# Turning the key-value sums: one transposition and two copies in place of two products and one copy

## The chip, the cores and the metric

The kernel runs on one core of a Trainium2 chip. A core has a matrix engine (TensorE, PE in the profile, with PEld for its weight loads), a vector engine (DVE), a scalar engine (ACT), GpSimd (POOL) and queues that start transfers (SP among them). The metric is the device time of one execution in microseconds (us), as the median of several. A profiled execution has besides a span, from the first to the last instruction of the program; everything read from the profile is measured inside that span.

## The reference, cut to what matters

Four batches, four heads, 1088 tokens, head dimension 32. Attention uses a feature map of 64 products (8 x 8) in place of a softmax, and the result goes through a two-layer network with an exact GELU:

```python
def phi(x):                       # 32 numbers -> 64 features
    a, b = S1 @ x, S2 @ x         # 8 and 8
    return outer(a, b).reshape(64)

kv  = einsum('bhsf,bhsd->bhfd', phi(k), v)      # 64 x 32 for each batch and head
z   = phi(k).sum(axis=tokens)
num = einsum('bhsf,bhfd->bhsd', phi(q), kv)
den = einsum('bhsf,bhf->bhs',  phi(q), z) + 1e-6
x   = (num / den)                               # heads side by side: 4352 x 128
out = gelu_exact(x @ w_in) @ w_out              # 128 -> 2048 -> 128
```

The change concerns `kv` of batches 1 to 3 between its summation and its use in `num`. No number that the reference defines is left out or altered.

## The kernel before, in words

The tokens are cut into nine pieces: for each batch two of 512 tokens (pieces 0 to 7), and one that gathers the last 64 tokens of every batch. For each piece the kernel computes query features, then the attention output, then for 16 slices of 128 hidden channels the first layer (L721), the GELU (L728, on ACT) and the second layer (L807). Most of the second layer is computed with a scheme that takes 7 products in place of 8; GpSimd forms sums of its inputs at L772 to L775, and L807 multiplies them.

In this long stage a hidden slice is two products (L721), one for 64 output channels each. The first writes PSUM partitions 0 to 63, the second 64 to 127, so each uses one half of the array's columns, and the two run side by side. The products of the second layer come in pairs in the same way. In the profile such products have the form 128\*64 (rows of weights by columns of weights); a product on the whole array has the form 128\*128. Each float32 product appears as two records, each with a weight load of its own; a transposition through the matrix engine (L333, L702) appears as one.

The key-value sums of batch b (1 to 3) are formed by `kv_sum` (L437), 128 rows (head and value channel) by 64 columns (features). `take_kv` (L462) copies them to SBUF as `kv_T[b]`. `turn_kv` then turns them: the result `kz[b]` has the features in the rows, twice, in rows 0 to 63 and again in rows 64 to 127, because the two halves of the tokens are multiplied from different rows in `attend_products` (L633). Before the change each copy of the turned block is a product of its own, with `kv_T[b]` as the weights and the identity matrix as the other operand: one product for PSUM partitions 0 to 63, one for 64 to 127. One ACT copy (L468) takes all 128 rows to `kz[b]`.

`turn_kv` runs three times, for batches 1, 2 and 3, some 3 to 20 us after the copy to `kv_T`. The order of all work is written out by hand: the loop over `steps` emits one hidden slice, then whatever `slots[t]` holds for this step (there `turn_kv` sits), then the second layer's products of `products[t]`. At the end of the program every instruction is tied to the one before it on its engine, so each engine keeps the order of the text. On PE, `turn_kv` stands between a pair of L721 and a pair of L807 in all three cases; on ACT, its copy stands between two GELUs. PSUM for hidden slices (`hps`) has two banks, the banks of `turn_kv` come from `wps`, two buffers of two banks each. `kz[b]` is read next by the products of L633, several us later.

Batch 0 goes another way (L930, a copy alone) and is not touched.

Of the kernel before, what the change touches and what calls it, by code (L numbers as in the profile page):

```python
# [16 lines left out]
def kernel(  # L17
# [18 lines left out]
    pe, dve, act, pool, sp = nc.tensor, nc.vector, nc.scalar, nc.gpsimd, nc.sync  # L36
    B, H, S, D = q.shape
    R = S1.shape[0]
    F = R * R
# [27 lines left out]
    def work_banks():  # L67

        return wps.tile([128, 2, CW], FP, name="w_ps")
# [10 lines left out]
    def out_bank():  # L80
        return ops.tile([128, CW], FP, name="o_ps")
# [137 lines left out]
    ident = big.tile([128, 128], FP, name="ident")  # L219
# [8 lines left out]
    kz = [big.tile([128, 128], FP, name=f"kz{b}") for b in range(B)]  # L228
# [229 lines left out]
    kv_T = {}  # L458
# [4 lines left out]

    def turn_kv(b, banks):

        for rows in (slice(0, 64), slice(64, 128)):
            pe.matmul(banks[rows, 1, :128], lhsT=kv_T[b], rhs=ident, start=True, stop=True)  # L467
        act.copy(out=kz[b], in_=banks[:, 1, :128])  # L468


    S_ab = big.tile([128, 2, 2 * R], FP, name="S_ab")
# [436 lines left out]
    banks = [out_bank(), out_bank()]  # L908
# [174 lines left out]
    at(24, kv_and_attend, 1, 1)  # L1083
    at(24, query_sketch, 2)
    at(26, lambda: turn_kv(1, held["kv"]))
    at(24, query_outer, 2)
    for i, t in enumerate((25, 26, 28)):
# [3 lines left out]
    for n in range(3, NCHUNK):  # L1091

        t = (n - 1) * NF
        b = (n + 1) // 2 if n % 2 else n // 2
        keys = n % 2 and b < B
        if n == NMAIN - 2:
            for m in (n, n + 1, NMAIN):
                at(t - 6, query_turn, m)
            at(t - 1, last_sketches, b)
            for i in range(2):  # L1100
                at(t + 6 + 3 * i, query_outer, n + i)
            at(t + 11, lambda b=b: turn_kv(b, work_banks()))
            at(t + NF - 1, last_attends)
# [4 lines left out]
        if keys:  # L1108
            at(t - 1, sketch_and_attend, n)
            at(t - 1, features_of_all, b)  # L1110
        else:
            if n % 2 == 0 and b < B:
                at(t - 1, z_sum, b)
                at(t - 1, fold_z, b)
                at(t - 1, kv_and_attend, b, n - 1)
                at(t + 1, lambda b=b: turn_kv(b, held["kv"]))
            else:
                at(t - 1, attend, n - 1)
            at(t - 1, query_sketch, n)
# [16 lines left out]
    for t, (n, fi) in enumerate(steps):  # L1136
# [13 lines left out]
        elif fi % NB == NB - 1:  # L1150
            b = fi // NB
# [11 lines left out]
    for t in range(len(steps) + LAG):  # L1163
        if t < 4:
# [9 lines left out]
            if t == 3:  # L1174
                banks = work_banks()
# [26 lines left out]
        if t < len(steps) and steps[t][0] < NMAIN and steps[t][1] % NB == NB - 1:  # L1202
            n, b = steps[t][0], steps[t][1] // NB
# [50 lines left out]
```

## Time and profile before

| what | value |
|---|---|
| time, median of 3 executions | 259.25 us (259.1 to 259.41) |
| span of the profiled execution | 257.9 us |
| granted TensorE clock over the span | 0.999 |
| L467, products of `turn_kv` | 12 records, 272 ns each, three places: 60.7, 103.0 and 176.1 us |
| L468, the ACT copy of `turn_kv` | 3 records, 259 ns each |
| L462, the ACT copy to `kv_T` | 3 records, 217 ns each |
| L721 on PE | 514 records, 136.9 us busy |
| L728 on ACT, blocks of 4 slices | 128 records, 73.1 us busy |

The span is shorter than the time by 1.4 us, which lie before the first and after the last instruction. A record of a matrix product is longer than the distance to the next one, since products are pipelined: its duration has the way through the array in it. What a product costs the engine is therefore read from the distance between starts, or from the chain of waits, which counts each stretch once. In the forms, "128\*64 128x512 f32" is a product with 128 rows and 64 columns of weights that 512 columns stream through. A merged row ("x4") covers several records that follow each other.

### The profile page before, as it was taken

To read this page: it belongs to the slowest core of one execution; us is meant where nothing else is said; L and a number is where in the kernel's file an instruction comes from. 1 tells how busy PE (TensorE), PEld (TensorE's weight loads), DVE (VectorE), ACT (ScalarE), POOL (GpSimd) and SP (SyncE) were. 2 spreads that over 40 slices of the span, in tenths; PEclk is the share of its full clock that TensorE was granted. 3 is DMA by queue.
4 is the path that set the end of the run, shared out by engine and by line. 5 is a ranking of instruction groups with operands and counts; after the bars stand their busy time and mean duration, and the time that the engine had idled before them with its cause. 6 is when DMAs were issued, how large, how long until landed. Compare 5 with 4: busy or idle time off the path is not lost.

```text
span 257.9 us, 5770 instructions
## 1 busy us (share of the span) xinstructions
PE 253.1 (98%) x2335; PEld 135.5 (53%) x2335; DVE 151.1 (59%) x313; ACT 115.2 (45%) x224; POOL 163.6 (63%) x173
## 2 busy tenths in 40 slices
PE   8989999999999999999999999999999999999995
PEld 7846444354444545444444455455544444445794
DVE  3786888969699997590178986399307000700330
ACT  4665777433626332543335332533444334433442
POOL 3313006799968778587758775787758777877300
PEclk9999999999999999999999999999999999999999
DMA  6459747751000101102000002000200200020020
GB/s 203 143 156 375 181 117 174 211 131 15 4 0 13 29 3 23 20 8 35 3 0 3 0 10 37 0 1 3 41 3 5 38 0 1 7 36 0 3 41 20
DMA packets 29594, 13.48 MB, mean 52 GB/s; under 512 B 21888, under 2 KB 27776, under 8 KB 29568
## 3 DMA queue, kind: packets, MB, share of 16 engines
q1 hardware_dynamic: 29392, 13.05, 20.2%
q8 instruction: 18, 0.29, 0.5%
q10 hardware_dynamic: 176, 0.07, 0.1%
q14 instruction: 8, 0.07, 0.1%
HBM read 10.88 MB, written 2.23 MB: 51 GB/s over the span
## 4 chain that ended last, share of the span: by engine, by line
PE 93%; SPq 2%; DMA 2%; DVE 1%; issue 0%; ACT 0%
PE h_ps L721 45%; PE o_ps L807 33%; PE o_ps L858 5%; PE w_ps L855 3%; DMA small<-in_moe_w_in_dram 2%; PE w_ps L437 1%; PE w_ps L578 1%; PE w_ps L633 1%; SPq L132 1%; PE h_ps L737 1%; SPq L100 1%; PE w_ps L977 1%; PE w_ps L656 0%; SPq L118 0%; PE w_ps L467 0%
## 5 line engine op out<-in xcount | busy, mean ns | idle before, releaser
L721 PE MATMUL h_ps<-xT,w_in 128*64 128x512 f32 (+3 forms) x514 | 136.9, 576 | 0.0
L728 ACT ACTIVATE block<-h_ps 128x512 f32<-128x512 f32 (+1 forms) x128 | 73.1, 571 | 117.2 <-PE h_ps L721 115.3
L721 PEld LDWEIGHTS h_ps<-xT,w_in 128*64 128x64 f32 (+1 forms) x514 | 41.9, 142 | 30.5 <-issue 11.6
L807 PE MATMUL o_ps<-block,w_out 128*64 128x256 f32 x224 | 57.5, 379 | 0.0
L772 POOL TENSOR_TENSOR bits_low<-block 128x512 f32<-128x512 f32 x28 | 36.0, 1286 | 27.7 <-ACT block L728 27.7
L807 PEld LDWEIGHTS o_ps<-block,w_out 128*64 128x64 f32 x224 | 30.5, 137 | 38.0 <-issue 27.5
L773 POOL TENSOR_TENSOR bits_a<-block 128x512 f32<-128x512 f32 x28 | 35.8, 1278 | 11.8 <-ACT block L728 11.8
L822 DVE COPY sums<-o_ps 64x256 f32<-64x256 f32 x8 | 3.3, 417 | 60.6 <-PE o_ps L807 60.6
L774 POOL TENSOR_TENSOR bits_e<-bits_a,block 128x512 f32<-128x512 f32 x28 | 36.1, 1288 | 2.2
L775 POOL TENSOR_TENSOR bits_m<-block,bits_e 128x512 f32<-128x512 f32 x28 | 35.9, 1282 | 2.2
L807 PE MATMUL o_ps<-bits_a,small 128*64 128x256 f32 x112 | 28.8, 379 | 0.0
L807 PE MATMUL o_ps<-bits_low,small 128*64 128x256 f32 x112 | 28.8, 379 | 0.0
L807 PE MATMUL o_ps<-block,small 128*64 128x256 f32 x112 | 28.8, 379 | 0.0
L807 PE MATMUL o_ps<-bits_m,w_out 128*64 128x256 f32 x112 | 28.7, 379 | 0.0
L807 PEld LDWEIGHTS o_ps<-block,small 128*64 128x64 f32 x112 | 15.2, 137 | 17.9 <-issue 10.8
L807 PE MATMUL o_ps<-bits_e,small 128*64 128x256 f32 x112 | 17.0, 383 | 0.0
L858 PE MATMUL o_ps<-g,w_out 128*128 128x512 f32 (+1 forms) x34 | 16.5, 572 | 0.0
L807 PEld LDWEIGHTS o_ps<-bits_m,w_out 128*64 128x64 f32 x112 | 15.3, 137 | 0.0
L807 PEld LDWEIGHTS o_ps<-bits_a,small 128*64 128x64 f32 x112 | 15.2, 137 | 0.0
L807 PEld LDWEIGHTS o_ps<-bits_low,small 128*64 128x64 f32 x112 | 15.2, 137 | 0.0
L590 DVE STREAM_TRANSPOSE w_ps<-w_ps 128x512 f32<-128x512 f32 (+1 forms) x7 | 4.8, 687 | 17.1 <-ACT xT L644 12.7
L807 PEld LDWEIGHTS o_ps<-bits_e,small 128*64 128x64 f32 x112 | 7.7, 137 | 10.6 <-issue 8.8
(195 smaller groups left out, 303.7 us busy)
## 6 DMA issues: line engine op xcount, KB each, us to landing
block<-in_moe_w_in_dram SPq DMA_DIRECT2D x3, 512.0 KB, 11.3
block<-in_moe_w_out_dram SPq DMA_DIRECT2D x3, 512.0 KB, 14.7
k<-in_k_dram SPq DMA_DIRECT2D x12, 128.0 KB, 2.9
v<-in_v_dram SPq DMA_DIRECT2D x12, 128.0 KB, 3.5
q<-in_q_dram SPq DMA_DIRECT2D x24, 64.0 KB, 2.1
out_dram<-oT SPq DMA_DIRECT2D x21, 64.0 KB, 2.2
k<-in_k_dram SPq DMA_DIRECT2D x2, 256.0 KB, 2.8
q<-in_q_dram SPq DMA_DIRECT2D x2, 256.0 KB, 3.9
```

The lines of the kernel that those rows point to most:

```text
L100: eng.dma_start(out=main[n, b][:, heads], in_=src_of[n][b, heads, 0:MAIN, :].rearrange("h (p j) d -> p h j d", j=J))
L590: dve.transpose(out=tok, in_=ps[:, :, :H2])
L721: pe.matmul(ps[rows, :W], lhsT=w[:, rows], rhs=xT[n][:, :W], start=True, stop=True)
L728: act.activation(out=g_of[n, fi][:, :W], in_=ps[:, :W], func=ACT.Gelu)
L772: pool.tensor_sub(out=s[3], in0=a11, in1=a21)
L773: pool.tensor_add(out=s[1], in0=a21, in1=a22)
L774: pool.tensor_sub(out=s[2], in0=s[1], in1=a11)
L775: pool.tensor_sub(out=s[4], in0=a12, in1=s[2])
L807: pe.matmul(acc[n][bank][half * 64:(half + 1) * 64, col:col + HW], lhsT=fixed, rhs=moving, start=opens and e == 0 and name in "4715", stop ...
L822: dve.tensor_copy(out=N[lo, 0, one], in_=a0[lo, one])
L855: pe.matmul(o_of[n][i][:, :128], lhsT=g[:, i * 128:(i + 1) * 128], rhs=w_tile(w_out_sb, fi), start=first, stop=final)
L858: pe.matmul(o_of[n][:, cols], lhsT=w_tile(w_out_sb, fi), rhs=g[:, cols], start=first, stop=final)
```

## The change

`turn_kv` makes the turned block once, by a transposition through the matrix engine into PSUM partitions 0 to 63, and ACT copies it twice, to rows 0 to 63 and to rows 64 to 127 of `kz[b]`. F is 64.

```diff
     def turn_kv(b, banks):
 
-        for rows in (slice(0, 64), slice(64, 128)):
-            pe.matmul(banks[rows, 1, :128], lhsT=kv_T[b], rhs=ident, start=True, stop=True)
-        act.copy(out=kz[b], in_=banks[:, 1, :128])
+        pe.transpose(banks[:F, 1, :128], in_=kv_T[b], identity=ident)
+        for rows in (slice(0, F), slice(F, 2 * F)):
+            act.copy(out=kz[b][rows], in_=banks[:F, 1, :128])
```

The places of the calls, their order on the engines, the banks and the transfers stay as they were. On PE two products become one transposition at each of the three places; on ACT one copy of 128 x 128 becomes two of 64 x 128. In the program as built, a product of 64 weight columns names two of the array's four groups of 32 columns; the transposition, with 64 weight columns too, names all four, as the transpositions of 128 columns do. It has one weight load and one matrix instruction.

## The prediction

> **What bounds the kernel now.** I read the page first, for the bound:
>
> ```profile
> span 257.9 us, 5770 instructions
> PE 253.1 (98%) x2335; PEld 135.5 (53%) x2335; DVE 151.1 (59%) x313; ACT 115.2 (45%) x224; POOL 163.6 (63%) x173
> PE 93%; SPq 2%; DMA 2%; DVE 1%; issue 0%; ACT 0%
> ```
>
> PE is busy for 98% of the span and makes up 93% of the chain that ended last. In the 40 slices of the span its digit is 9 (90% or more) from the fourth to the last but one, so what is taken from its stream or put into it should reach the end one for one. ACT, at 45%, has room. Next the chain of waits around the first turn, 58 to 64 us (start, us, what):
>
> ```profile
> 59.18 0.86 PE o_ps L807 x8
> 60.04 0.86 PE h_ps L721 x4
> 60.90 0.22 PE w_ps L467 x4
> 61.12 0.86 PE o_ps L807 x8
> ```
>
> The turn, four records, costs 0.22 us of the chain. That is two passes of 0.11 us: the two products lie on different column halves and run side by side. The chain around the other turns has the same 0.22. No time is lost on either side, since L721, L467 and L807 all have the form 128\*64.
>
> The third view is PE's timeline where that form changes (96.2 to 100.6 us), and the chain there:
>
> ```profile
> 96.67 1.03 PE L721 MATMUL h_ps<-xT,w_in 128*64 128x512 f32 x4
> 97.63 0.32 PE L437 MATMUL w_ps<-k_s,ones 128*32 128x64 f32 x8
> ...
> 99.34 0.64 PE L578 MATMUL w_ps<-qT,S_abc 64*32 64x256 f32 x16
> 99.91 0.65 PE L807 MATMUL o_ps<-bits_e,small 128*64 128x256 f32 x4
> 100.39 0.60 PE L721 MATMUL h_ps<-xT,w_in 128*64 128x512 f32 x2
> ```
>
> ```profile
> 99.55 0.43 PE w_ps L578 x16
> 99.98 0.58 PE o_ps L807 x4
> ```
>
> A block of four L721 records takes 0.86 in the chain, so L437 could start at 96.67 + 0.86 = 97.53; it starts at 97.63. I read the 0.10 us as the array running empty before it takes another division of its columns. After L578, the four records of L807 cost 0.58 in the chain, where eight cost 0.86 and so four 0.43: 0.15 us more. Of these, 0.05 is the first weight load, which nothing hides (99.91 to 100.39 is 0.48, not 0.43; a first L807 record is 430 ns where the median is 379), and 0.10 is the emptying again.
>
> Last, transpositions, by line and in the timeline:
>
> ```profile
> L333 PE MATMUL w_ps<-ident,q x4: 272/272/328, 10.9 to 11.2; 128*128 128x128 f32 x4
> L333 PE MATMUL o_ps<-ident,k_rem x1: 328/328/328, 8.5 to 8.5; 128*128 128x128 f32 x1
> ```
>
> ```profile
> 8.52 0.33 PE L333 MATMUL o_ps<-ident,k_rem 128*128 128x128 f32 x1
> 8.78 0.66 PE L426 MATMUL o_ps<-sums,k_p 128*64 128x33 f32 x16
> ...
> 21.41 0.38 PE L702 MATMUL w_ps<-ident,x_tok 128*128 128x128 f32 x2
> 21.63 0.60 PE L858 MATMUL o_ps<-g,w_out 128*128 128x256 f32 x2
> ```
>
> Among whole-array neighbours two transpositions cost 21.63 - 21.41 = 0.22, so one costs 0.11 and being a transposition costs nothing more. Between products on halves (8.52), one holds PE for 8.78 - 8.52 = 0.26 from its start. The first one after a change of form is 328 ns instead of 272: 0.056 of weight load in the open.
>
> **The change part by part.** Removed on PE: at each of three places the stretch of 0.22 us, with its four loads and passes. Added: one load and one transposition with 128 moving columns. A pass of its own is 0.11 (the 21.41 row).
>
> What else it costs depends on the form it runs in. No row before shows a float32 transposition on half of the columns, so I bound it. If it shared the form of its neighbours, it would take 0.11 on one half and the turn would save 0.22 - 0.11 = 0.11. If it takes the whole array, as every transposition in this trace does, PE must change form before and after:
>
> - emptying after L721: 0.10 (the L437 row)
> - its weight load in the open: 0.056 if it costs what 128 columns cost (328 - 272), 0.028 if it halves with 64 columns
> - its pass: 0.11
> - emptying before L807: 0.10
> - the first load of L807 in the open: 0.05
>
> That is 0.39 to 0.42, against 0.22: 0.17 to 0.20 more per turn. The distances of 0.10 are read from hundredths and may be 0.09, which takes the low end to 0.15. The sandwich at 8.52 agrees: 0.26 after its start, with 0.10 before it and 0.05 behind it, is 0.41. I take the whole array, because the built instruction names all four column groups, and 0.18 per turn, between the ends: 3 x 0.18 = 0.54 us, with bounds 0.45 and 0.60.
>
> One rule of the Trainium skill speaks against this change: "TensorEngine Tiling (Array Packing)", Restrictions under Tile-to-Partition Mapping, says that column tiling rules out the transpose mode for float32 input. No run here shows it. By it the sum is the loss of 0.54 just made; were it not to hold on this chip, the sum would be the gain of 3 x 0.11 = 0.33.
>
> On ACT one copy more at each place. The one copy of 128 x 128 takes 0.26 (259 ns); a copy's time should go by its 128 columns, not its rows, so I take 0.26 for each of two, bounded below by 0.24 (the 64x64 copies of L503 take 238 ns) and above by 0.58 (64 x 512, L819). What stands behind it is the next GELU:
>
> ```profile
> 176.80 0.26 ACT L468 COPY kz<-w_ps 128x128 f32<-128x128 f32 x1
> 177.87 0.60 ACT L728 ACTIVATE block<-h_ps 128x512 f32<-128x512 f32 x1 [0.81 <-PE h_ps L721]
> ```
>
> It waits 0.81 us for L721, and 1.19 at the other two places (62.89 and 105.13 us). One more copy, even at 0.58, fits into that, so I cost it at nothing. Without this cover it would delay a GELU by 0.26, and POOL's sums (L772) after it; PE would feel that only when the hidden bank came back late. The reader of `kz`, L633, comes at 68.6 us or later for a turn at 60.7, so nobody waits for the second copy. DVE, POOL, SP and the transfers have the same instructions in the same order, and no queue is passed.
>
> The sum against the profiled execution: 257.9 + 0.54 = 258.4 us of span. The median before is 259.25, 1.4 above the span for the part outside it; that part is not touched. So 259.25 + 0.54 = 259.79 us.
>
> **The rivals.**
>
> *The transposition shares its neighbours' form.* Each turn saves 0.11: 259.25 - 0.33 = 258.92 us, faster. For it: it has 64 weight columns as they have, and L702 shows that switching to a transposition is free where the form stays. Against it: it names four column groups, and every transposition in the trace is 128\*128. It decides if the change of form at both ends costs less than the pass saved, below 0.11 per turn.
>
> *It changes nothing.* The change of form is partly hidden, say one emptying instead of two and loads under cover: 0.11 + 0.10 = 0.21, against 0.22. Time 259.25. For it: one product fewer to issue. Against it: the trace shows the emptying on both sides of a different form, on the way in at 97.63 and on the way out at 99.91.
>
> *The emptying is longer around a transposition.* A record of 272 ns with a pass of 0.11 leaves 0.16 us on the way through the array. If PE waits for all of it before and after, each emptying is 0.16 instead of 0.10: 0.12 more per turn, 0.36 in all, 259.79 + 0.36 = 260.15. For it: the gap before 8.52 may be a little above 0.10. Against it: 8.78 - 8.52 has 0.06 load and 0.11 pass in it, which leaves 0.09 for the way out.
>
> *ACT becomes the bound at the turns.* It would take a delay of more than 0.81 us from one copy, above the dearest row of 0.58; I give it no chance of its own.
>
> **How the numbers follow.** A difference of 0.2% (0.52 us) is about what a measurement of this kernel can tell from no change. The whole-array case gets 0.78, from 0.45 to 0.60 us, that is 259.70 to 259.85; the line at 259.77 runs through it. Since the sandwich sums to the upper part, I put 0.56 above the line and 0.22 below. The longer emptying gets 0.07, all slower. The shared form gets 0.10; at -0.33 it is within the line, with 0.03 for a measurement that falls beyond it. No change gets 0.05. Slower: 0.56 + 0.07 = 0.63. Same: 0.22 + 0.07 + 0.05 = 0.34. Faster: 0.03. The predicted time is the whole-array case's, 259.79. Its own range with the scatter before (0.16 us to either side) is 259.55 to 260.0; for 8 in 10 over all cases I take 259.45 to 260.05, which leaves out the shared form, no change and most of the longer emptying.
>
> **What would show each step.** In the changed profile the new line's record should have the form 128\*64 or 128\*128 with 328 or some 300 ns, not 272; L721 to the transposition should be 0.86 + 0.10 between starts, and the transposition to L807 about 0.23 to 0.27; the first L807 record after it should be 430 ns. The chain should show some 0.4 us per turn for the transposition and the excess of L807 together. ACT should show six copies of about 0.26, with the GELU after them still waiting for L721. Records of 272 ns with L807 0.11 behind would prove the shared form; a GELU that starts right behind the second copy with L721 long done would prove ACT. A difference far from three equal steps at 60, 103 and 176 us would make this account wrong.

## The result, and the profile after

| | before | after |
|---|---|---|
| median of 22 executions | 259.36 us | 259.82 us |
| ratio, with its 95% interval | | 1.0018 (1.0011 to 1.0025) |
| span of the profiled execution | 257.9 us | 257.9 us |

The change makes the kernel slower by 0.46 us. One execution of each kernel was far longer (680.57 us before, 332.25 after); the ratio leaves them out. The difference is real, as the interval lies above 1; the ratio is just under the line of 0.2%, and its interval reaches past it. The two spans are equal all the same, and that is the first thing to understand. A span holds the start of the run too, where the first loads land sooner or later. In the profile before, the first record of the key-value sums (L437), which stands ahead of all three turns, starts at 55.34 us, in the one after at 54.92: this execution was 0.42 us ahead before any turn had run. PE's timelines, before and then after:

```profile
55.34 0.32 PE L437 MATMUL w_ps<-k_s,ones 128*32 128x64 f32 x8
243.07 1.50 PE L855 MATMUL w_ps<-w_out,block 128*128 128x128 f32 x12
```

```profile
54.92 0.32 PE L437 MATMUL w_ps<-k_s,ones 128*32 128x64 f32 x8
243.14 1.50 PE L855 MATMUL w_ps<-w_out,block 128*128 128x128 f32 x12
```

From there to the first product of the closing part (the first L855 record, at 243.07 and 243.14) it takes 187.73 us before and 188.22 after: 0.49 us more. I use this stretch below, because the starting time has dropped out of it.

The page of the changed kernel, first lines:

```profile
span 257.9 us, 5755 instructions
PE 253.6 (98%) x2326; PEld 134.8 (52%) x2326; DVE 151.0 (59%) x313; ACT 115.8 (45%) x227; POOL 163.2 (63%) x173
```

PE has nine records fewer (3 in place of 12) and ACT three more. The shares are as before, but for one point less of PEld.

The chain of waits around the first turn (start, us, what):

```profile
59.62 0.86 PE h_ps L721 x4
60.48 0.23 PE w_ps L466
60.71 1.01 PE o_ps L807 x8
61.72 0.86 PE h_ps L721 x4
```

From the start of the L721 block to the start of the next it takes 61.72 - 59.62 = 2.10 us; before it was 61.98 - 60.04 = 1.94. The turn costs 0.16 us more. The other two show the same: 2.10 against 1.94 (102.03 to 104.13, before 102.28 to 104.22) and 1.67 against 1.51 (175.31 to 176.98, before 175.40 to 176.91). Three of them make 0.48. It isn't all on the turn's own line: that went from 0.22 to 0.23 only. The rest sits on L807, whose block takes 1.01 instead of 0.86. Who reads only the changed line finds no loss.

PE's timeline shows the pieces. First the pair of L807 behind the turn and the next one, before:

```profile
60.95 0.38 PE L807 MATMUL o_ps<-block,small 128*64 128x256 f32 x1
61.16 0.38 PE L807 MATMUL o_ps<-block,small 128*64 128x256 f32 x1
```

and after:

```profile
59.45 1.03 PE L721 MATMUL h_ps<-xT,w_in 128*64 128x512 f32 x4
60.41 0.30 PE L466 MATMUL w_ps<-ident,kv_T 128*64 128x128 f32 x1
60.64 0.43 PE L807 MATMUL o_ps<-block,small 128*64 128x256 f32 x1
60.65 0.43 PE L807 MATMUL o_ps<-bits_low,small 128*64 128x256 f32 x1
60.91 0.38 PE L807 MATMUL o_ps<-block,small 128*64 128x256 f32 x1
```

L721 is through at 59.45 + 0.86 = 60.31; the transposition starts at 60.41, 0.10 later. L807 follows 0.23 behind it, where the pass alone is 0.11. Its first pair lasts 0.43 us instead of 0.38, and the next pass comes 0.27 later instead of some 0.22: what the prediction calls the weight load in the open. The form is printed as 128\*64, since it counts the weight columns in use; only the gaps on both sides tell that the transposition does not share its neighbours' form.

Such a gap needs no transposition. At the end of the long stage of the kernel before, an ordinary product on the whole array follows products on halves:

```profile
242.23 0.38 PE L807 MATMUL o_ps<-bits_m,w_out 128*64 128x256 f32 x1
242.54 0.70 PE L721 MATMUL h_ps<-xT,w_in 128*128 128x256 f32 x2
```

Pairs of L807 follow each other at some 0.22, so L721 could start near 242.44; it starts 0.10 later. The GELU that it waits for, by its semaphore, had been over since 242.27.

By line, the transposition and the two copies:

```profile
L466 PE MATMUL w_ps<-ident,kv_T x3: 299/299/300, 60.4 to 176.1; 128*64 128x128 f32 x3
```

```profile
L468 ACT COPY kz<-w_ps x6: 247/252/257, 61.0 to 177.0; 64x128 f32<-64x128 f32 x6
```

299 ns is neither the 272 of a transposition among its like nor the 328 of one of 128 columns after a change of form. And at the tightest place for ACT, the third turn, its timeline reads:

```profile
176.70 0.52 ACT L468 COPY kz<-w_ps 64x128 f32<-64x128 f32 x2
177.94 0.60 ACT L728 ACTIVATE block<-h_ps 128x512 f32<-128x512 f32 x1 [0.72 <-PE h_ps L721]
```

The GELU behind the two copies still waits 0.72 us for L721.

### The profile page after: what moved, and what is told of

Read it like the earlier page. It is cut to its first block, busy times and chain, and to the rows that moved or that the text cites. A ratio compares the mean times of both kernels' runs of the same rounds, so it can differ in the third digit from the quotient of the medians.

```text
span 257.9 us, 5755 instructions
## 1 busy us (share of the span) xinstructions
PE 253.6 (98%) x2326; PEld 134.8 (52%) x2326; DVE 151.0 (59%) x313; ACT 115.8 (45%) x227; POOL 163.2 (63%) x173
## 4 chain that ended last, share of the span: by engine, by line
PE 96%; DMA 2%; SPq 0%; DVE 0%; issue 0%; ACT 0%
PE h_ps L721 45%; PE o_ps L807 33%; PE o_ps L858 5%; PE w_ps L855 3%; DMA q<-in_q_dram 2%; PE w_ps L437 1%; PE w_ps L578 1%; PE w_ps L633 1%; PE w_ps L543 1%; PE o_ps L426 1%; PE h_ps L737 1%; PE w_ps L977 1%; PE w_ps L656 0%; SPq L100 0%; PE w_ps L333 0%; DVE qT L528 0%
## 5 line engine op out<-in xcount | busy, mean ns | idle before, releaser
L721 PE MATMUL h_ps<-xT,w_in 128*64 128x512 f32 (+3 forms) x514 | 136.9, 576 | 0.0
L721 PEld LDWEIGHTS h_ps<-xT,w_in 128*64 128x64 f32 (+1 forms) x514 | 41.8, 142 | 30.5 <-issue 11.8
L807 PE MATMUL o_ps<-block,w_out 128*64 128x256 f32 x224 | 57.5, 379 | 0.0
L807 PEld LDWEIGHTS o_ps<-block,w_out 128*64 128x64 f32 x224 | 30.5, 137 | 38.1 <-issue 27.6
L807 PE MATMUL o_ps<-block,small 128*64 128x256 f32 x112 | 28.9, 380 | 0.0
L807 PE MATMUL o_ps<-bits_low,small 128*64 128x256 f32 x112 | 28.9, 380 | 0.0
L807 PE MATMUL o_ps<-bits_a,small 128*64 128x256 f32 x112 | 28.8, 379 | 0.0
L807 PE MATMUL o_ps<-bits_m,w_out 128*64 128x256 f32 x112 | 28.7, 379 | 0.0
L807 PEld LDWEIGHTS o_ps<-block,small 128*64 128x64 f32 x112 | 15.1, 137 | 18.1 <-issue 10.8
L807 PE MATMUL o_ps<-bits_e,small 128*64 128x256 f32 x112 | 17.1, 384 | 0.0
L807 PEld LDWEIGHTS o_ps<-bits_m,w_out 128*64 128x64 f32 x112 | 15.3, 137 | 0.0
L807 PEld LDWEIGHTS o_ps<-bits_a,small 128*64 128x64 f32 x112 | 15.2, 137 | 0.0
L807 PEld LDWEIGHTS o_ps<-bits_low,small 128*64 128x64 f32 x112 | 15.1, 137 | 0.0
L807 PEld LDWEIGHTS o_ps<-bits_e,small 128*64 128x64 f32 x112 | 7.6, 137 | 10.8 <-issue 8.8
```

The source lines that it names most:

```text
L721: pe.matmul(ps[rows, :W], lhsT=w[:, rows], rhs=xT[n][:, :W], start=True, stop=True)
L807: pe.matmul(acc[n][bank][half * 64:(half + 1) * 64, col:col + HW], lhsT=fixed, rhs=moving, start=opens and e == 0 and name in "4715", stop ...
```

## The experiments

The theory: the transposition takes the whole array while its neighbours hold half of it each, so PE pays two changes of form per turn. The rivals: the second copy on ACT, a transposition that shares its neighbours' form, and scatter at the head of the run. The table has medians with the ratio to the kernel before on the same chip; "stretch" is from the first L437 record to the first L855 record in the profile, against 187.73 us before. The ratio is not the quotient of the two medians: in runs 2 and 10, each with one execution of 262.21 us, it is larger by 0.0013 and 0.0012.

| run | median us | before | ratio (95%) | stretch us |
|---|---|---|---|---|
| 1 two copies alone | 259.27 | 259.41 | 0.9996 (0.9981 to 1.001) | 187.73 |
| 2 one transposition of 128 columns | 259.82 | 259.41 | 1.0029 (1.0011 to 1.0047) | 188.30 |
| 3 two turns off PE | 259.54 | 259.41 | 1.0004 (0.9993 to 1.0014) | 187.81 |
| 4 the change again | 259.99 | 259.41 | 1.0023 (1.0012 to 1.0034) | 188.22 |
| 5 in alternation | 266.23 | 259.41 | 1.0271 (1.0241 to 1.0301) | 194.93 |
| 6 in groups | 264.4 | 259.41 | 1.0201 (1.015 to 1.0252) | 192.47 |
| 7 first turn moved | 259.58 | 259.41 | 1.0005 (0.9992 to 1.0018) | 188.07 |
| 8 two turns off PE, staged | 258.85 | 259.55 | 0.9975 (0.9963 to 0.9987) | 187.30 |
| 9 three turns off PE, staged | 258.39 | 259.55 | 0.9961 (0.9949 to 0.9973) | 187.07 |
| 10 loads later alone | 259.29 | 259.43 | 1.0007 (0.9988 to 1.0027) | 187.73 |
| 11 as 9, again | 258.87 | 259.43 | 0.9983 (0.997 to 0.9996) | 187.07 |

### 1: two copies, the products kept

```diff
-        act.copy(out=kz[b], in_=banks[:, 1, :128])
+        for rows in (slice(0, F), slice(F, 2 * F)):
+            act.copy(out=kz[b][rows], in_=banks[rows, 1, :128])
```

> The two products stay, and ACT copies the turned block in two copies of 64x128 instead of one of 128x128. If the loss is the matrix engine's change of form around the transposition, this costs nothing: within 0.15 us of the kernel before, ratio 0.9994 to 1.0006, with six ACT records of about 0.25 us and 0.22 us of PE per turn. If the loss is the second copy on ACT, which holds back a GELU, it shows here in full: about +0.46 us, ratio 1.0018.

The stretch is 187.73 us, to the hundredth that of the kernel before, and the interval of the ratio ends at 1.001, short of 1.0018. The second copy costs nothing that shows; its record is 254 ns. That rival is out.

### 2: one transposition of 128 columns, one copy

```diff
-        kv_T[b] = att.tile([128, F], FP, name="kv_T")
-        act.copy(out=kv_T[b], in_=ps[:, :F])
+        kv_T[b] = att.tile([128, 2, F], FP, name="kv_T")
+        act.copy(out=kv_T[b], in_=ps[:, None, :F].broadcast_to([128, 2, F]))
...
-        for rows in (slice(0, 64), slice(64, 128)):
-            pe.matmul(banks[rows, 1, :128], lhsT=kv_T[b], rhs=ident, start=True, stop=True)
+        pe.transpose(banks[:, 1, :128], in_=kv_T[b].rearrange("p s f -> p (s f)"), identity=ident)
         act.copy(out=kz[b], in_=banks[:, 1, :128])
```

> The copy to kv_T writes the 64 columns twice, one transposition of 128 columns turns both at once, and ACT makes one copy. Change of form theory: emptying 0.096, load 0.056 (record 328 ns, as for 128 columns before), pass 0.107, emptying 0.094, first load of L807 0.047, together 0.40 per turn against 0.22: +0.18 each, +0.54 us in all, ratio 1.002, a little above the changed kernel. If the second copy on ACT is the cause: no difference from before, ratio 1.000. If the changed kernel's record of 299 ns has nothing to do with the number of weight columns, the record here is 299 ns too.

By line:

```profile
L466 PE MATMUL w_ps<-ident,kv_T x3: 327/327/328, 60.2 to 175.9; 128*128 128x128 f32 x3
```

The stretch grew by 0.57 us, with one copy on ACT and openly on the whole array. Twice the weight columns make the record 28 ns longer (327 against 299), so the open load goes by the columns: 0.056 us for 128, 0.027 for 64. Three times 0.028 is 0.08, the distance of the two stretches (188.30 and 188.22).

### 4: the change again

> The changed kernel once more, beside the three others on the same chip. Change of form theory: 3 x (0.096 + 0.028 + 0.107 + 0.094 + 0.047 - 0.218) = 3 x 0.154 = +0.46 us, ratio 1.0018. If the difference was scatter at the head of the run, ratio 1.000 here.

The ratio comes back as 1.0023, and the stretch as 188.22, the same as in the first profile. It is not scatter.

### 5 and 6: twelve transpositions more, in alternation and in groups

```diff
-        for rows in (slice(0, 64), slice(64, 128)):
-            pe.matmul(banks[rows, 1, :128], lhsT=kv_T[b], rhs=ident, start=True, stop=True)
...
+        for i in range(4):
+            products()
+            turned()
+        products()
```

`products` is the pair that was there, `turned` the transposition of the change. In groups, four `turned` come first and then five `products`.

> Each turn makes its pair of products five times with a transposition between one pair and the next, nine steps in place of one; the last pair's result is used. Change of form theory: 12 more transpositions at 0.37 us (emptying, load, pass, emptying, first load behind it) and 12 more pairs at 0.22 us: +7.1 us in all. If a transposition with 64 weight columns shares its neighbours' form, a step of transposition and pair is 0.11 + 0.21 us: +3.9 us, and no gap of 0.1 us stands around any of them.

> The same twelve transpositions and twelve extra pairs, but per turn four transpositions in a row, then five pairs. Change of form theory: one change to the whole array and one back per turn: 0.37 us for the first transposition, 0.11 for each of three more, 0.22 for each of four more pairs, 1.57 per turn, +4.7 us in all; 2.4 us less than with the same work in alternation. If the form is shared, the order makes no difference: +3.9 us as in alternation.

PE's timeline in the first turn, in alternation (here L730 is L721, L816 is L807, L471 the products and L467 the transposition):

```profile
60.19 0.39 PE L471 MATMUL w_ps<-ident,kv_T 128*64 128x128 f32 x4
60.51 0.30 PE L467 MATMUL w_ps<-ident,kv_T 128*64 128x128 f32 x1
60.74 0.44 PE L471 MATMUL w_ps<-ident,kv_T 128*64 128x128 f32 x4
61.11 0.30 PE L467 MATMUL w_ps<-ident,kv_T 128*64 128x128 f32 x1
```

and in groups:

```profile
59.36 1.03 PE L730 MATMUL h_ps<-xT,w_in 128*64 128x512 f32 x4
60.32 0.63 PE L467 MATMUL w_ps<-ident,kv_T 128*64 128x128 f32 x4
60.87 1.31 PE L471 MATMUL w_ps<-ident,kv_T 128*64 128x128 f32 x20
62.02 0.38 PE L816 MATMUL o_ps<-block,small 128*64 128x256 f32 x1
```

In alternation one round of transposition and pair is 61.11 - 60.51 = 0.60 us; the expected sum was 0.37 + 0.22. In groups four transpositions take 60.87 - 60.32 = 0.55, the last emptying and one open load among it, which leaves some 0.11 for each. The same instructions cost 194.93 - 187.73 = 7.20 us in the one order and 192.47 - 187.73 = 4.74 in the other, where 7.1 and 4.7 were expected. A shared form would have given 3.9 in both. So the price belongs to the change between transposition and products, not to the transposition itself. That it is a change of the array's form, and not of the operation, rests on rows where one comes without the other: L721 at 242.54 pays the 0.10 with no transposition near it, and L702 pays nothing among whole-array products, on its way in (21.63 to 22.06 us, 0.43 for two records of 256 columns) as on its way out (22.06 to 22.28, 0.22 for two transpositions). A run with an ordinary whole-array product in the turn's place was not made. The medians, from two executions each, are 6.8 and 5.0 above the kernel before and agree in order.

### 7: the first turn behind L578

```diff
-    at(26, lambda: turn_kv(1, held["kv"]))
+    at(24, lambda: turn_kv(1, held["kv"]))
     at(24, query_outer, 2)
```

> The changed kernel with the first turn moved forward, to right behind L578, where the array changes form anyway. Change of form theory: of the first turn's 0.37 us the emptying and the first load behind it are paid by that change already, so it adds 0.096 + 0.028 + 0.107 = 0.23 us, 0.14 us less than in the changed kernel; the other two turns keep 0.37. The time, 0.14 us below the changed kernel, is too near to tell; the starts in the profile decide: L578's last pass to the transposition about 0.09, from the transposition to L807 0.23. If the cost were the transposition's own, not its place, the first turn would take 0.37 us here as well. If kv_T is late, PE waits for ACT in front of the transposition.

```profile
56.12 0.67 PE L578 MATMUL w_ps<-qT,S_abc 64*32 64x256 f32 x16
56.72 0.30 PE L466 MATMUL w_ps<-ident,kv_T 128*64 128x128 f32 x1
56.95 0.43 PE L807 MATMUL o_ps<-block,w_out 128*64 128x256 f32 x1
```

The stretch is 188.07, 0.15 less than with the change, as expected: one emptying and one open load are shared with a change that was there. Even in this place the transposition adds 0.23 us, no less than the pair of products, so this place doesn't win either. The medians don't tell this run from either kernel.

### 3 and 8 to 11: the turns taken off the matrix engine

If PE bounds everything here, then no form of the turn on PE is the best one. VectorE turns blocks of 32x32, and small transfers put the blocks where they belong. In run 3 they go straight to `kz`, 16 for each of batches 2 and 3:

```diff
+        if b > 1:
+            turned = att.tile([128, 2 * D], FP, name="kv_turned")
+            dve.transpose(out=turned, in_=kv_T[b])
+            for h in range(H):
+                for j in range(2):
+                    for s in range(2):
+                        rows = slice(s * F + j * D, s * F + (j + 1) * D)
+                        sp.dma_start(out=kz[b][rows, h * D:(h + 1) * D], in_=turned[h * D:(h + 1) * D, j * D:(j + 1) * D])
+            return
...
-            at(t + 11, lambda b=b: turn_kv(b, work_banks()))
+            at(t + 2, turn_kv, b, None)
```

> Batches 2 and 3 are turned without the matrix engine: VectorE transposes kv_T in blocks of 32x32, and 16 small transfers put the blocks in place. Batch 1 keeps its two products. If PE bounds everything at the turns, each 0.22 us taken off it reaches the end: -0.44 us, ratio 0.9983. If the transfers land late (more than 20 us after the turn of batch 2, or behind the stores of the same queue), L633 waits for them and the time rises, by more than 1 us. If PE's stream has slack elsewhere, ratio 1.000.

Neither expectation came true: the stretch is 187.81, as if nothing had been saved. PE's timeline at 125 us says why (L587, L642, L986, L816 are L578, L633, L977, L807):

```profile
125.17 0.66 PE L587 MATMUL w_ps<-qT,S_abc 64*32 64x256 f32 x16
125.63 0.94 PE L642 MATMUL w_ps<-q_pT,kz 64*32 64x256 f32 x14
126.20 0.44 PE L986 MATMUL w_ps<-kT,S_ab 64*32 64x256 f32 x5
126.28 0.37 PE L642 MATMUL w_ps<-q_pT,kz 64*32 64x256 f32 x1
...
127.14 0.65 PE L816 MATMUL o_ps<-bits_e,small 128*64 128x256 f32 x4
```

From L587 to L816 it takes 1.97 us; before, 1.46:

```profile
126.10 0.66 PE L578 MATMUL w_ps<-qT,S_abc 64*32 64x256 f32 x16
127.56 0.65 PE L807 MATMUL o_ps<-bits_e,small 128*64 128x256 f32 x4
```

The transfers had been issued by 117 us and landed 1.7 us after their issue (median; 3.4 at most, of those whose landing the trace tells), long before. What is new is that L642 has waits of its own for its blocks' transfers: between 125.19 and 126.09 us the trace has eight semaphore instructions of 51 ns on this line, where the kernel before has none. Its products don't start side by side any more, and the group grows by 0.51 us, more than the 0.44 saved. Run 8 tests that. The eight blocks go to a tile of their own, and two ACT copies, later on, take that to both halves of `kz`:

```diff
...
+    def place_kv(b):
+        for rows in (slice(0, F), slice(F, 2 * F)):
+            act.copy(out=kz[b][rows], in_=held["staged", b])
...
```

> As the third experiment, but for batches 2 and 3 the eight transferred blocks land in a tile of their own, and two ACT copies bring them to kz, so that L633 waits for ACT as before and not for eight transfers. If those waits in front of L633 gave back what the turn saved in the third experiment, L587 to L986 at 125 us shrinks from 1.97 to 1.46 us and the whole gain arrives: 2 x 0.22 = -0.44 us, ratio 0.9983. If it was something else about the transfers, the time stays at 1.000.

```profile
125.54 0.66 PE L591 MATMUL w_ps<-qT,S_abc 64*32 64x256 f32 x16
126.00 0.64 PE L646 MATMUL w_ps<-q_pT,kz 64*32 64x256 f32 x16
126.43 0.64 PE L990 MATMUL w_ps<-kT,S_ab 64*32 64x256 f32 x16
127.00 0.65 PE L820 MATMUL o_ps<-bits_e,small 128*64 128x256 f32 x4
```

The group, from L591 to L820 (its end, where the expectation names L986), is back at 1.46 us with no semaphore instruction in it, the stretch is 187.30, 0.43 below the kernel before, and the time is 0.9975 of it (0.9963 to 0.9987, with the expected 0.9983 inside). Run 9 does the same for all three batches; for the first, the loads of L128 make room on the queue (`at(40, load_q_rem)`), and the copies come at step 29.

> The same for all three batches; the loads of the last tokens' queries (L128) go behind the first eight of these transfers on their queue, since they are needed much later. If PE bounds everything and the transfers land in time (by 64 us for the first, read at 68 us): 3 x 0.22 = -0.65 us, ratio 0.9975. If the first turn's transfers are late, L633 at 68 us waits and the gain is lost or turned round.

> The ninth experiment once more, beside the tenth on the same chip. If only the three turns taken off PE count: 187.08 us between the first L437 and the tail in the trace, 0.65 us less than before, ratio 0.9975. If the ninth's 0.9961 was more than scatter at the head of the run, it comes back.

> The kernel before, with nothing changed but the loads of the last tokens' queries (L128) behind the first 16 stores on their queue, as in the ninth experiment. If those loads touch nothing that PE waits for, ratio 1.000. If the ninth experiment's gain beyond 0.65 us came from them, ratio near 0.9985 here.

Both profiles of the three turns off PE have a stretch of 187.07 us, 0.66 below before: 3 x 0.22, and the first turn's transfers were in time. The first ratio, 0.9961, was better than that explains (0.9975), the second, 0.9983 (0.997 to 0.9996), a little worse. The loads moved alone change nothing (187.73, interval from 0.9988 to 1.0027). I put the difference between runs 9 and 11 down to scatter at the start. The profiled executions of these two, which are the same kernel, reach the first record of the key-value sums at 56.06 and 54.98 us and have the same stretch behind it, so the start alone moves single executions by 1.08 us; that it moved the medians is not shown. This version is faster than the kernel before in both runs; the changed kernel was not run beside it.

## Why the prediction was right, point by point

- *PE bounds the kernel, and what is put into its stream reaches the end.* Right: 0.16 us per turn in the chain, 0.49 in the stretch, 0.46 in the medians; and 0.66 less in the stretch when the turns left PE.
- *The transposition takes the whole array, with two changes of form.* Right in its price, which runs 5 and 6 show best, as only the order differs between them. The division itself stands in no record; it is inferred from the gaps and from the rows at 242.54 and 22.06 us. What the array does in the 0.10 us that I called emptying, no run shows.
- *The terms.* Emptying before, 0.10: measured 0.10. First load of L807, 0.05: measured 0.05 (0.43 against 0.38). The transposition's own load was bounded by 0.028 and 0.056, for 64 and for 128 columns: it is the low one, 0.027. With that, and distances that round a little high, the turn costs 0.16 more, not the 0.18 I took. Three of them make 0.48 to 0.49 instead of 0.54. This is the one size that was off, and it decides on which side of 0.2% the time falls: I had put most of the chance above the line, and the ratio came out at 1.0018, below it. The measurement told more finely than the 0.2% I had allowed for: its interval is 0.0007 to either side.
- *The second copy is hidden.* Right: run 1, and the GELU that still waits for L721.
- *The rivals.* The shared form and the case of no change fall by runs 5 and 6, where each transposition between halves costs 0.38 (0.60 - 0.22) and not 0.11 or 0.22. The longer emptying falls by the timeline: 0.10 in front, not 0.16. ACT falls by run 1.
- *The rule of the Trainium skill.* "TensorEngine Tiling (Array Packing)", Restrictions under Tile-to-Partition Mapping, rules out the transpose mode with column tiling for float32. The runs agree with what it leads to: with 64 weight columns the transposition pays for leaving the half-array form and coming back, at every place tried. A float32 transposition on half of the array was not tried.

The forecast time was 259.79 us, the measured one 259.82. That they agree to 0.03 is luck, since the median before had moved by 0.11 as well; the difference forecast was 0.54, the one measured 0.46.

## What to carry to other kernels

Price an instruction on TensorE by where it stands: a transposition that costs 0.11 us among whole-array products costs 0.38 between products on halves, and more than half of the extra is booked on the line of the products behind it (0.15 on L807). Two concurrent half-array products that write both copies at once can beat one transposition that needs half the passes. Where PE bounds, compare stretches between fixed products, not spans of single executions: the start of the run moved by 0.42 us between the two profiles here, nearly the whole effect, and by 1.08 between runs 9 and 11.

## What the runs showed of the hardware that was not expected

Waits for transfers that have long landed are not free on PE if they stand between products that would run side by side: the same 48 records of L578, L633 and L977 took 1.97 us instead of 1.46 when L633 waited for the blocks' transfers separately. At 183 us in the same run, where L633 is the first group behind L721, such waits cost nothing that shows: the eight semaphore instructions are over by 181.1 us, while products of the step before run, and the group starts at 182.23 and takes 1.41 us to L807, as before (182.86 to 184.27).

The open weight load of a transposition (28 ns for each 64 columns) is about half of that of a float32 product: a first L807 record, with 64 columns, is 0.05 us longer than the others.
